# Preparing an LSH-masked attention two head pairs at a time, with one chain of scales and one hash compare for both

## The chip, the cores and the metric

The kernel runs on one core of a Trainium2 chip. That core has a matrix engine (TensorE, PE in the profile; its weight loads are listed apart as PEld), a vector engine (VectorE, DVE), a scalar engine (ScalarE, ACT), a general engine (GpSimd, POOL), and a sync engine (SyncE, SP), from whose queue nearly all transfers are issued, one behind the other. The metric is the time of one execution on the device in microseconds (us); the median of three runs is what counts.

## The reference

Two parts stand one behind the other: attention in which a query sees only the keys of its own hash bucket, and a feed-forward layer on what the attention gives.

```python
q_bits = (np.einsum('bhsd,dk->bhsk', q, proj) > 0)          # B,H,S,D = 4,8,768,64 ; 6 bits
k_bits = (np.einsum('bhsd,dk->bhsk', k, proj) > 0)
mask   = (bucket of q)[:, :, :, None] == (bucket of k)[:, :, None, :]
scores = np.matmul(q, k.transpose(0, 1, 3, 2)) / np.sqrt(64)
scores = np.where(mask, scores, -1000000000.0); scores -= max over keys
attn   = exp(scores) / (sum of exp + 1e-09)
x      = (attn @ v) as [3072, 512]
h      = x @ w_in                                            # 512 -> 2048
g      = np.where(h > 0.0, h, np.exp(np.minimum(h, 0.0)) - 1.0)
out    = g @ w_out                                           # 2048 -> 512
```

q, k, v and proj are float32; w_in and w_out are handed over as 64-bit words, from which the kernel makes float32.

## The kernel before

**Numbers in two halves.** A float32 operand is scaled by a power of two and split into a high and a low float16 part, and a product is made of two or three float16 matmuls. The high part is written by ACT (`scaled`, line 143), the low part by DVE (`rest`, line 152). The power of two comes from the largest squared norm of the tile: ACT makes the squares with their sum (`squares`, line 207), and `powers` turns the maximum over the partitions into an exponent and its reciprocal in four or five DVE operations on one or two columns (lines 186 to 199).

**Pairs, chunks and slots.** The 8 heads of a batch are taken as 4 pairs. A batch has two chunks of 384 queries, so there are 8 chunks of 4 pairs, and a pair of a chunk has 6 score tiles of 128 queries by 768 keys ("slots", 24 to a chunk). A slot is: scores on PE (`s`, line 508; in the start every second one is `so`), their maximum and copy to `pt` on DVE (520), the exponentials of two slots on ACT (536), whose bias `nb` comes from POOL (533), the division and split of the probabilities (`hl`, ACT 143 and DVE 152), a transposing transfer into `PT`. When a pair of a chunk has its six tiles, 36 matmuls `av` (560) multiply with V's halves `vhl`, and ACT and DVE write `x` (569, 570).

**Preparing a pair.** `prep` gives the steps of a group of pairs: load (SP, `kst` and `qst`), squares, scales, split, project. The split writes the halves of K into `natk` and of Q into `nat1q`/`nat2q`, and issues the transposing transfers (K at 328, `O1`/`O2` of Q at 371 and 372). The project step copies K's halves to a second tile (`dup`, line 162), multiplies K or Q with the six hash vectors (`z`, line 286), compares the result with a threshold (`zb`, DVE, line 291), and sends the bits by four or two small transfers beside the transposed halves, where the score matmuls pick them up. K is prepared once per batch, with the batch's first chunk; in the second chunk a group has Q alone. From chunk 1 on a group has two pairs. In batch 0's first chunk, a group is one pair; there the buffers of the pairs are three `Stage`s, the first in buffers of its own, the others in the tail of the large tile `W`, as long as no decoded weight stands there. From then on all pairs share one `natk`, `nat1q` and `nat2q`.

**What sets the order.** The list `due` gives each step a slot at which it is to be written: so many slots ahead of the group's first slot (`PREP`, and `PREP0` in the start), not before the step of the group ahead that frees its buffers. Within a slot, the order in the program is scores, exponentials, due steps, weights, feed-forward. Each engine works its own list in order. The order on PE is as written from slot 30 on; for the others a scheduler places what is ready by its own estimate. `behind_max` ties a small DVE operation behind the last score maximum.

**Feed-forward.** A stream of 16 steps per chunk runs six slots behind the attention: `h` (PE 587), Exp and Relu (ACT 600, 602), their combination (DVE 610), the split of `g` into two halves (`U<-U,sgg`, ACT 143 and DVE 152), the second product `o` (PE 630). When a chunk ends, its three 128x512 results leave PSUM as `W<-o,os` and `W<-o_1556,os` (ACT 143; one by DVE 145) into two output areas, and POOL's queue sends them out. The next chunk's `o` takes the same PSUM banks.

**Weights.** 32 slabs of 128x512 are loaded as 64-bit words, decoded (ACT 143, DVE 468, 469, 479), and their column maximum is gathered on PE (`acc`, line 472). When all 16 of a matrix are there, each slab is split (`W<-W,w0s` and `W<-W,w1s`, ACT 143 and DVE 152). All of it is put between the steps of batch 0, and a decode that would overwrite a spare stage buffer waits until the pair that uses it is through.

## Time and profile before

| | |
|---|---|
| median of 3 runs | 938.73 us (935.84, 938.73, 945.27) |
| span of the profiled execution | 936.1 us; it is the only time that this execution has |
| busy share | PE 87%, DVE 76%, ACT 75%, POOL 10% |
| instructions | 14723 |
| mean granted TensorE clock | 0.933 |
| read from and written to HBM | 35.65 MB and 6.29 MB |

The page of the profile gives busy times, a map of the span in 40 slices, the chain of work that ended last, and the costliest groups of instructions. A group's row has the line, the engine, the operation, what is written from what (partitions x elements and type), the count, the total busy time in us with the mean of one in ns, and the engine's idle time just ahead of it with what ended most of that. A row of a timeline has the start, the duration, the instruction, and in brackets the idle time ahead of it with its releaser. A row of the waits has the engine and its line, the releaser, the total in us, the number of times, the longest. The two batches of numbers at a row's end in the table by stretches are the granted clock, the DMA share and GB/s.

### The profile page before, as it was taken

How to read it: one execution, taken by the hardware profiler on the slowest of the kernel's cores; microseconds unless marked ns; L12 is line 12 of the kernel's file. 1: busy time of each engine (PE TensorE's matmuls, PEld its weight loads, DVE VectorE, ACT ScalarE, POOL GpSimd, SP SyncE). 2: the span in 40 equal slices, each digit the busy share in tenths (PEclk: the TensorE clock that was granted, in tenths of full speed). 3: DMA queues.
4: the chain of work that ended last, by engine and by line, in shares of the span. 5: the costliest groups of instructions: out<-in, count | busy, mean ns of one | idle time of the engine just before them, and what ended most of it. 6: DMA issues, size and time to landing. Idle time of an engine off the chain costs nothing.

```text
span 936.1 us, 14723 instructions
## 1 busy us (share of the span) xinstructions
PE 817.0 (87%) x4975; PEld 419.3 (45%) x4975; DVE 712.8 (76%) x1624; ACT 705.4 (75%) x1277; POOL 97.4 (10%) x145
## 2 busy tenths in 40 slices
PE   2436655899898999999988999999999999999996
PEld 0113222354443555554544554455445555555553
DVE  7899889898975868788975777788888787775332
ACT  5666685898968777878877877789787788775442
POOL 1000000011111110210111010200111102110000
PEclk9956665899998999999999999999999999999998
DMA  9999987669787678798798758697687767665000
GB/s 290 270 220 212 232 223 177 120 131 180 137 144 175 133 119 134 148 158 183 138 194 147 146 99 139 147 174 151 118 182 131 120 119 153 103 108 96 34 1 35
DMA packets 404588, 138.49 MB, mean 148 GB/s; under 512 B 380960, under 2 KB 398880, under 8 KB 404512
## 3 DMA queue, kind: packets, MB, share of 16 engines
q1 hardware_dynamic: 402432, 131.25, 70.8%
q0 software_dynamic: 1920, 6.29, 2.1%
q8 instruction: 39, 0.64, 0.3%
q14 instruction: 37, 0.30, 0.1%
q10 hardware_dynamic: 160, 0.00, 0.0%
HBM read 35.65 MB, written 6.29 MB: 45 GB/s over the span
## 4 chain that ended last, share of the span: by engine, by line
PE 36%; issue 12%; DVE 8%; DMA 6%; ACT 5%; POOL 1%; SPq 1%; POOLq 0%; DVEq 0%; ACTq 0%
PE o L630 12%; PE h L587 11%; PE s L508 6%; PE av L560 5%; DVE pt L520 3%; DMA K<-natk 3%; DVE hl L152 2%; ACT pt L536 1%; POOL nb L533 1%; PE z L286 1%; DMA kst<-in_k_dram 1%; ACT hl L143 1%; DMA PT<-hl 1%; DMA out_dram<-W 1%; ACT U L143 1%
## 5 line engine op out<-in xcount | busy, mean ns | idle before, releaser
L630 PE MATMUL o<-W,U 128*128 128x512 f16 x1152 | 284.4, 384 | 13.3 <-ACT W L143 10.5
L587 PE MATMUL h<-x,W 128*128 128x384 f16 x1536 | 279.9, 326 | 0.0
L536 ACT ACTIVATE pt<-pt,nb,sg 128x768 f32<-128x768 f32 x192 | 195.3, 1020 | 53.4 <-POOL nb L533 52.7
L152 DVE SCALAR_TENSOR_TENSOR hl<-pt,r,hl 128x768 f16<-128x768 f32 x192 | 190.6, 1012 | 15.4 <-ACT hl L143 15.2
L587 PEld LDWEIGHTS <-W 128*128 128x128 f16 x1536 | 147.6, 98 | 111.4 <-issue 10.3
L143 ACT ACTIVATE hl<-pt,r 128x768 f16<-128x768 f32 x192 | 168.3, 925 | 15.5 <-issue 6.7
L520 DVE TENSOR_SCALAR_CACHE_REDUCE pt<-s 128x768 f32<-128x768 f32 x177 | 168.2, 950 | 14.0 <-issue 5.5
L630 PEld LDWEIGHTS <-U 128*128 128x128 f16 x1152 | 111.5, 98 | 137.0 <-issue 21.2
L508 PE MATMUL s<-K,O 128*128 128x384 f16 x708 | 153.6, 340 | 21.7 <-DVE pt L520 14.8
L533 POOL TENSOR_SCALAR nb<-m,sg 128x2 f32<-128x2 f32 x96 | 81.5, 849 | 716.5 <-DVE pt L520 376.9
L152 DVE SCALAR_TENSOR_TENSOR U<-U,sgg 128x384 f16<-128x384 f32 x128 | 78.7, 615 | 70.4 <-ACT U L143 69.7
L508 PEld LDWEIGHTS <-O 76*128 76x128 f16 (+1 forms) x768 | 74.4, 102 | 121.9 <-issue 47.5
L143 ACT ACTIVATE U<-U,sgg 128x384 f16<-128x384 f32 x128 | 77.8, 608 | 59.3 <-DVE U L610 59.3
L560 PE MATMUL av<-PT,vhl 128*64 128x384 f16 x1152 | 111.9, 347 | 11.8 <-DMA PT<-hl 6.4
L560 PEld LDWEIGHTS <-vhl 128*64 128x64 f16 x1152 | 71.2, 116 | 61.2 <-issue 17.5
L610 DVE SCALAR_TENSOR_TENSOR U<-U 128x384 f32<-128x384 f32 x128 | 70.7, 553 | 36.6 <-ACT U L602 36.6
L600 ACT ACTIVATE U<-h,ch 128x384 f32<-128x384 f32 x128 | 72.4, 566 | 32.0 <-PE h L587 31.9
L602 ACT ACTIVATE U<-h,ch 128x384 f32<-128x384 f32 x128 | 72.7, 568 | 0.0
L472 PE MATMUL acc<-W,ones 128*128 128x512 bf16 x32 | 17.6, 557 | 39.2 <-DVE W L469 37.4
L570 DVE SCALAR_TENSOR_TENSOR x<-av,x 128x384 f16<-128x384 f32 x32 | 17.7, 555 | 30.4 <-ACT x L569 30.4
L536 ACT ACTIVATION_READ_ACCUMULATOR pt<-pt,nb,sg 128x1 f32 x192 | 36.4, 190 | 0.0
L291 DVE TENSOR_SCALAR zb<-z,pjt 64x384 f16<-64x384 f32 (+1 forms) x48 | 29.0, 604 | 0.3 <-PE z L286 0.3
(103 smaller groups left out, 521.1 us busy)
## 6 DMA issues: line engine op xcount, KB each, us to landing
U<-in_moe_w_in_dram SPq DMA_DIRECT2D x12, 512.0 KB
vf<-in_v_dram SPq DMA_DIRECT2D x16, 384.0 KB
U<-in_moe_w_out_dram SPq DMA_DIRECT2D x12, 512.0 KB
out_dram<-W POOLq DMA_DIRECT2D x24, 256.0 KB, 3.7
qst<-in_q_dram SPq DMA_DIRECT2D x30, 192.0 KB
kst<-in_k_dram SPq DMA_DIRECT2D x14, 384.0 KB
PT<-hl SPq DMA_TRANSPOSE x192
W<-in_moe_w_in_dram SPq DMA_DIRECT2D x4, 512.0 KB
```

Of the source, the lines that this page charges most:

```text
L143: nc.scalar.activation(o, x, AF.Copy, scale=s)
L152: nc.vector.scalar_tensor_tensor(o, x, s, hi, ALU.mult, ALU.subtract)
L508: nc.tensor.matmul(s_tile[:, n, :HALF], st[o][:rows, at, :], kst[kk][:rows, j * NC + n * HC : j * NC + (n + 1) * HC, :].rearrange("p a b - ...
L520: top = nc.vector.tensor_scalar(pt.rearrange("p (n e) -> p n e", n=2), s_tile[:, :, :HALF], CLAMP, None, ALU.max, ALU.max, accum_out=duo[0 ...
L533: nc.gpsimd.tensor_scalar(nb[:, :w], m[:, :w], st["sg"][:, 1:2], 1.0, ALU.mult, ALU.mult)
L536: nc.scalar.activation(pt, pt, AF.Exp, bias=nb[:, n : n + 1], scale=st["sg"][:, 0:1], accum_out=sm[:, n : n + 1])
L560: nc.tensor.matmul(av[j * D : (j + 1) * D], vt[:, j, c, vx, :], PTs[j][:, :, px, c, :], start=n == 0, stop=n == last,)
L587: nc.tensor.matmul(h, WH[:, g * KT + t, wx, fc * P : (fc + 1) * P], c["xs"][t][:, xx, :], start=n == 0, stop=n == 3 * KT - 1,)
L600: nc.scalar.activation(e, h, AF.Exp, scale=c["ch"])
L602: nc.scalar.activation(hp, h, AF.Relu, scale=c["ch"])
L610: nc.vector.scalar_tensor_tensor(e, e, -1.0, hp, ALU.add, ALU.min)
L630: nc.tensor.matmul(o[t][:, :DO], g16[:, gx, t * P : (t + 1) * P], WH[:, NSI + 1 + f, wx, :], start=f == 0 and i == 0, stop=f == NF - 1 and ...
```

## The change

Four things change in how pairs are prepared.

1. The steps of preparation are regrouped: groups are of two pairs from the start, in batch 0 too, and there are four stages instead of three. Both pairs of a group are split at the same due slot (as far as the ring of three Q buffers lets them), K is still projected pair by pair, Q once for both.
2. K's and Q's scales of a group come from one chain, `qk_scales`: six DVE operations for K and Q of both pairs (five where only Q is prepared), instead of two chains and two products. The factors 2^64 go into the constants; the negative scale is no longer made, POOL multiplies by -1 instead.
3. The hash bits of Q of two pairs are compared in one operation on 128 partitions (before: two on 64). The four small transfers behind it are as before.
4. V's halves are written for two heads in one operation (768 columns, before: two of 384).

```diff
-STAGES = 3
+STAGES = 4
...
-            d = nc.sync.dma_start(o[D : D + 2 * NB, u * w : (u + 1) * w], zb[u * QD : u * QD + 2 * NB])
+            d = nc.sync.dma_start(o[u], zb[u * QD : u * QD + 2 * NB])
...
+        def project():
             w = nc_ * P
+            hi, lo, o = [], [], []
+            for st in sts:
+                o1, o2 = flat(st["O1"]), flat(st["O2"])
+                for u in range(2):
+                    at = slice(u * w, (u + 1) * w)
+                    hi.append(o1[:, at])
+                    lo.append(o2[:D, at])
+                    o.append(o2[D : D + 2 * NB, at])
+            bits(o, ((2, hi), (2, lo), (3, lo)), w, 1)
...
+    def qk_scales(b, ps, mx, kw, ksts, qsts):
+        w = len(ps)
+        n = kw + w
+        mall = small.tile([P, 4], F32, tag="qkm", name="qkm")[:, :n]
+        if kw:
+            t = ps_a.tile([P, 512], F32, tag="av", name="sum")[:, :kw]
+            nc.tensor.matmul(
+                t, ones, mx[:, :kw].bitcast(BF16).rearrange("p (n t) -> p n t", t=2)[:, :, 1], start=True, stop=True
+            )
+            nc.vector.tensor_scalar(mall[:, :kw], t, 4.0, None, ALU.max)
+        nc.vector.tensor_scalar(mall[:, kw:], mx[:, kw:], 4.0, None, ALU.max)
+        ex = small.tile([P, 4], F32, tag="ke" if kw else "qe", name="qke", bufs=4 if kw else 2)[:, :n]
+        nc.vector.tensor_scalar(
+            ex.bitcast(I32), mall.bitcast(I32), 1, 0x7F800000, ALU.logical_shift_right, ALU.bitwise_and
+        )
+        sc = small.tile([P, 4], F32, tag="qks", name="qks")[:, :n]
+        nc.vector.reciprocal(sc, ex)
+        nc.vector.tensor_scalar(sc, sc, 2.0 ** (QK_TOP - 64), None, ALU.mult)
+        sg = small.tile([P, 2], F32, tag="sg", name="sg")
+        c = D**-0.5 * 2.0 ** (128 - 2 * QK_TOP)
+        nc.vector.scalar_tensor_tensor(sg[:, :w], ex[:, kw:], c, kexs[b, ps[0]], ALU.mult, ALU.mult)
...
-            for j in range(2):
-                scaled("v_hi", t[:, j, :, 0, :], f[:, j], st["sc"])
-                rest("v_lo", t[:, j, :, 1, :], f[:, j], st["sc"], t[:, j, :, 0, :])
+            scaled("v_hi", t[:, :, :, 0, :], f, st["sc"])
+            rest("v_lo", t[:, :, :, 1, :], f, st["sc"], t[:, :, :, 0, :])
...
-        nc.gpsimd.tensor_scalar(nb[:, :w], m[:, :w], st["sg"][:, 1:2], 1.0, ALU.mult, ALU.mult)
+        nc.gpsimd.tensor_scalar(nb[:, :w], m[:, :w], st["sg"], -1.0, ALU.mult, ALU.mult)
...
-    groups = [[n] for n in range(NP)] + [[n, n + 1] for n in range(NP, len(pairs), 2)]
+    groups = [[n, n + 1] for n in range(0, len(pairs), 2)]
...
-            at = begin[n] - (PREP0 if early else PREP)[2]
+            at = lead[2]
...
+        a = max(split_at[0], scale_at)
         for i, n in enumerate(ns):
+            a = max(a, split_at[i])
+            due.append((a, n, 2, lambda split=split, i=i: split(i)))
+        z = max(lead[3], a)
+        for i, p in enumerate(projects):
+            due.append((z + i, ns[-1], 3 + i, p))
```

The steps move, and with them what stands between others on each engine. Three places show it; line numbers of the changed kernel are larger by up to 19 in what follows the new function.

The first place is ACT's list at the end of chunk 0 (its feed-forward's last step), from just ahead of the first copy out of PSUM (`W<-o,os`) or a little behind it, to the last (`W<-o_1556` and `W<-o_1494`). `natk,kx<-kst` and `nat1q,qx<-qst` (`qkx` in the changed kernel) are the squares of K and Q of batch 1's first group. Before:

```order
L143 ACTIVATE U<-U,sgg 128x384
L207 ACTIVATE nat1q,qx<-qst 128x384
L600 ACTIVATE U<-h,ch 128x384
L602 ACTIVATE U<-h,ch 128x384
L207 ACTIVATE natk,kx<-kst 128x768
L207 ACTIVATE nat1q,qx<-qst 128x384
L600 ACTIVATE U<-h,ch 128x384
L602 ACTIVATE U<-h,ch 128x384
L143 ACTIVATE hl<-pt,r 128x768 x2
L207 ACTIVATE natk,kx<-kst 128x768
L143 ACTIVATE U<-U,sgg 128x384
L143 ACTIVATE W<-o_1556,os 128x512
```

And of the changed kernel, the same stretch:

```order
L207 ACTIVATE nat1q,qkx<-qst 128x384 x2
L143 ACTIVATE U<-U,sgg 128x384
L143 ACTIVATE hl<-pt,r 128x768 x2
L616 ACTIVATE U<-h,ch 128x384
L618 ACTIVATE U<-h,ch 128x384
L143 ACTIVATE W<-o,os 128x512
L552 ACTIVATE pt,sm<-pt,nb,sg 128x768 x2
L143 ACTIVATE U<-U,sgg 128x384
L616 ACTIVATE U<-h,ch 128x384
L618 ACTIVATE U<-h,ch 128x384
L143 ACTIVATE W<-o_1494,os 128x512
```

K's squares no longer stand between the copies: they come some ten exponentials later, Q's stand ahead of the first copy, and one pair of Exp and Relu and the two `hl` halves have left the stretch.

The second place is SP's queue in the start, from the first pair's transposes to the load of V. `K_209` (`K_204`) and `O_215`, `O_216` (`O_210`, `O_211`) are the first pair's transposed halves, `O_321`, `O_322`, `K_315` (`O_235`, `O_236`, `K_229`) the second pair's, `K_210<-zb` (`K_205`) the first pair's hash bits; `W<-in_moe` and `U<-in_moe` are slabs of weights. Before:

```order
L372 DMA_TRANSPOSE O_216<-nat2q 128x6x128
L371 DMA_TRANSPOSE O_215<-nat1q 128x6x128
L328 DMA_TRANSPOSE K_209<-natk 128x12x128
L456 DMA W<-in_moe_w_in_dram 128x1024
L456 DMA U<-in_moe_w_in_dram 128x1024 x3
L305 DMA kst<-in_k_dram 128x2x384
L372 DMA_TRANSPOSE O_322<-W 128x6x128
L295 DMA K_210<-zb 12x384 x4
L391 DMA vf<-in_v_dram 128x2x384 x4
L456 DMA W<-in_moe_w_in_dram 128x1024
```

And of the changed kernel:

```order
L353 DMA_TRANSPOSE O_211<-nat2q 128x6x128
L320 DMA_TRANSPOSE K_204<-natk 128x12x128
L472 DMA W<-in_moe_w_in_dram 128x1024
L352 DMA_TRANSPOSE O_210<-nat1q 128x6x128
L472 DMA U<-in_moe_w_in_dram 128x1024 x3
L320 DMA_TRANSPOSE K_229<-W 128x12x128
L352 DMA_TRANSPOSE O_235<-W 128x6x128
L353 DMA_TRANSPOSE O_236<-W 128x6x128
L295 DMA K_205<-zb 12x384 x4
L408 DMA vf<-in_v_dram 128x2x384 x4
```

The second pair's three transposes now all stand ahead of the first pair's bits and of V, where one stood before.

The third place is DVE's list in the preparation of a batch with loads from the shared buffers (batch 2's first pair), from K's low half (`natk<-kst`) to the copy of its transposed halves (`K_4220<-K_4219`, then `K_4079<-K_4078`), which can start only when the transposing transfer has landed. Before:

```order
L152 SCALAR_TENSOR_TENSOR natk<-kst,ks,natk 128x12x64
L520 TENSOR_SCALAR pt,m<-s 128x768
L546 TENSOR_SCALAR r<-sm 128x2
L152 SCALAR_TENSOR_TENSOR U<-U,sgg 128x384
L152 SCALAR_TENSOR_TENSOR nat2q<-qst,qs,nat1q 128x6x64
L547 RECIPROCAL r<-r 128x2
L162 COPY nat1q<-nat1q 128x6x64
L520 TENSOR_SCALAR pt,m<-s 128x768
L610 SCALAR_TENSOR_TENSOR U<-U 128x384
L408 TENSOR_REDUCE vx_4260<-vx 128x1
L152 SCALAR_TENSOR_TENSOR hl<-pt,r,hl 128x768 x2
L162 COPY K_4220<-K_4219 64x1536
```

And of the changed kernel:

```order
L152 SCALAR_TENSOR_TENSOR natk<-kst,qks,natk 128x12x64
L536 TENSOR_SCALAR pt,m<-s 128x768
L152 SCALAR_TENSOR_TENSOR nat2q<-qst,qks,nat1q 128x6x64
L162 COPY nat1q<-nat1q 128x6x64
L626 SCALAR_TENSOR_TENSOR U<-U 128x384
L152 SCALAR_TENSOR_TENSOR hl<-pt,r,hl 128x768 x2
L536 TENSOR_SCALAR pt,m<-s 128x768
L162 COPY K_4079<-K_4078 64x1536
```

The split of `g`, the maximum of V and the two small operations on `r` no longer stand between the two.

More of the change, by code (lines that the diff above doesn't have):

```diff
@@ L333, in project @@
             quads = [k1[:, u * HALF : (u + 1) * HALF] for u in range(4)]
-            st["done"] = bits(k2, ((0, quads), (1, quads)), HALF, 0)
-        return load, scale, split, project
+            o = [k2[D : D + 2 * NB, u * HALF : (u + 1) * HALF] for u in range(4)]
+            st["done"] = bits(o, ((0, quads), (1, quads)), HALF, 0)
+        return load, sums, split, project
     def prep_q(b, c0, nc_, ps, ksts, sts, sgs):
@@ L347, in load, with sums @@
                     )
-        def scale():
-            w = len(ps)
-            mx = small.tile([P, 2], F32, tag="qx", name="qx")[:, :w]
+        def sums(mx):
             for n, (st, sg_) in enumerate(zip(sts, sgs)):
                 squares(mx[:, n : n + 1], flat(st["qf"]), sg_.q1[:, : 2 * nc_])
-            yield
-            ex, sc = powers(mx, w, 4.0, QK_TOP, "q", rows=True, squares=True)
-            sg = small.tile([P, 2, 2], F32, tag="sg", name="sg")
-            c = D**-0.5 * 2.0 ** (-2 * QK_TOP)
-            for x in range(2):
-                nc.vector.scalar_tensor_tensor(
-                    sg[:, x, :w], ex, c if x == 0 else -c, kexs[b][:, ps[0] : ps[0] + w], ALU.mult, ALU.mult
-                )
-            for n, st in enumerate(sts):
-                st["qsc"], st["sg"] = sc[:, n : n + 1], sg[:, :, n]
         def split(st, sg_):
@@ L717, in prep @@
         made = []
+        kw = len(ps) if c["c0"] == 0 else 0
         def sums():
-            made.extend(part[1]() for part, _ in parts)
-            for m in made:
-                next(m)
+            mx = small.tile([P, 4], F32, tag="qkx", name="qkx")[:, : kw + len(ps)]
+            made.append(mx)
+            if kw:
+                parts[0][0][1](mx[:, :kw])
+            parts[-1][0][1](mx[:, kw:])
         def scale():
             with behind_max():
-                for m in made:
-                    next(m, None)
+                qk_scales(b, ps, made[0], kw, ksts, [qs[n] for n in ns])
         def split(i):
@@ L731, in split @@
                 part[2](sts[i], sgs[i])
-        def project(x, i):
-            part, sts = parts[x]
-            part[3](sts[i])
-        return load, sums, scale, split, project, len(parts)
+        projects = [lambda st=st: parts[0][0][3](st) for st in ksts] if kw else []
+        projects.append(parts[-1][0][3])
+        return load, sums, scale, split, projects
     due = []
```

45 lines of the change are left out of this document (17 added, 28 removed).

## The prediction

> **What bounds the kernel.** I read the page first, then the table of busy time by stretches, then the waits of PE and DVE, then the timeline where a wait is long. The stretches are the start, and then roughly the feed-forward of each chunk; the columns are busy time (and count) of PE, PEld, DVE, ACT and POOL, then the granted clock, the DMA share and GB/s.
>
> ```profile
> span 936.1 us, 14723 instructions
> ...
> 0.00:165.00 165.00, 84.30 (x374) 34.94 (x375) 145.18 (x370) 108.02 (x192) 9.13 (x39) 0.70 0.93 230
> 165.00:283.00 118.00, 106.62 (x659) 54.15 (x658) 101.03 (x232) 101.68 (x183) 16.62 (x14) 0.96 0.77 145
> 283.00:385.00 102.00, 97.62 (x614) 51.36 (x612) 74.63 (x164) 82.02 (x154) 9.97 (x14) 0.97 0.76 142
> ...
> 690.00:790.00 100.00, 99.81 (x640) 52.78 (x639) 77.70 (x173) 79.31 (x145) 11.57 (x16) 1.00 0.75 139
> 790.00:936.00 146.00, 138.22 (x825) 73.38 (x823) 70.42 (x131) 82.82 (x146) 10.71 (x15) 0.98 0.32 62
> ```
>
> From 283 on PE is busy 96 to 100% of a stretch: PE's work bounds it, and a saving on DVE or ACT moves nothing there unless PE waits for it. In the first 165 us PE is busy for half of the time; DVE is busy 145.18 of 165 and the DMA engines 0.93, so this stretch is bounded by DVE, with the transfers close behind. The stretch from 165 to 283 lies between: PE is without work for 118 - 106.62 = 11.4 us. So a change to the preparation can pay in three places: the start, the first chunk, and single waits of PE later.
>
> ```profile
> PE acc L472 <- DVE W L469: 37.4, 16, 5.8
> ...
> PE o L630 <- ACT W L143: 10.5, 4, 4.6
> ...
> DVE K L162 <- DMA K<-natk: 13.2, 10, 3.5
> ```
>
> The first row is the start (column maxima behind weight decodes). The second is PE waiting for the copy that frees the PSUM bank of `o` when a chunk ends: 10.5 us in four places. The third is DVE standing before the copy of K's transposed halves.
>
> **The change part by part: the ends of chunks 0 and 2 (-11).** The timeline at the end of chunk 0, ACT's and PE's rows:
>
> ```profile
> 283.88 0.67 ACT L143 ACTIVATE W<-o,os 128x512 f32<-128x512 f32 x1
> ...
> 288.63 0.84 ACT L207 ACTIVATE natk<-kst 128x768 bf16<-128x768 f32 x1
> 288.84 1.46 PE L630 MATMUL o<-W,U 128*128 128x512 f16 x6
> ...
> 290.90 1.75 ACT L143 ACTIVATE hl<-pt,r 128x768 f16<-128x768 f32 x2
> 292.55 0.83 ACT L207 ACTIVATE natk<-kst 128x768 bf16<-128x768 f32 x1
> 293.88 0.67 ACT L143 ACTIVATE W<-o,os 128x512 f32<-128x512 f32 x1
> 294.61 2.72 PE L630 MATMUL o<-W,U 128*128 128x512 f16 x6 [4.30 <-ACT W L143]
> 297.25 4.16 PE L560 MATMUL av<-PT,vhl 128*64 128x384 f16 x36
> ```
>
> ACT makes four squares, four Exp and Relu and two `hl` halves between its two copies, so the second comes 10 us behind the first, and PE stands for 4.30 us. The six matmuls behind it take 2.72 us where six take 1.46 otherwise, and the 36 `av` 4.16 where a chain row has 3.05:
>
> ```profile
> 292.00:294.00 2.00, 0.00 (x0) 0.00 (x0) 1.81 (x2) 2.00 (x5) 0.00 (x0) 0.65 1.13 243
> 294.00:296.00 2.00, 1.39 (x4) 0.55 (x4) 0.73 (x2) 2.00 (x4) 0.59 (x1) 0.50 0.48 109
> 296.00:298.00 2.00, 2.00 (x10) 0.61 (x9) 0.00 (x0) 1.97 (x5) 0.00 (x0) 0.50 0.42 145
> ...
> 345.81 3.05 PE av L560 x36
> ```
>
> The granted clock falls to 0.50 behind the wait: 1.26 us lost on `o` and 1.11 on `av`. At the end of chunk 2 the same stands, here because the square waits for its load:
>
> ```profile
> 492.64 0.84 ACT L207 ACTIVATE natk<-kst 128x768 bf16<-128x768 f32 x1 [1.84 <-DMA kst<-in_k_dram]
> ...
> 498.11 2.72 PE L630 MATMUL o<-W,U 128*128 128x512 f16 x6 [4.61 <-ACT W L143]
> ```
>
> Together 4.30 + 1.26 + 1.11 + 4.61 + 1.26 = 12.5 us. In the changed order K's squares come behind the last copy, and what is left between the copies is one pair of exponentials, one of Exp and Relu, one split. That is what the kernel before has at the end of chunk 1:
>
> ```profile
> 385.16 0.68 ACT L143 ACTIVATE W<-o,os 128x512 f32<-128x512 f32 x1
> ...
> 391.33 0.69 ACT L143 ACTIVATE W<-o,os 128x512 f32<-128x512 f32 x1 [0.85 <-DMA out_dram<-W]
> ...
> 392.07 1.45 PE L630 MATMUL o<-W,U 128*128 128x512 f16 x6 [0.26 <-ACT W L143]
> ```
>
> There the copies are 6.2 us apart, PE waits 0.26 us, and `o` runs at full speed. The fourth of the waits, at the end of chunk 3, is 10.5 - 4.30 - 4.61 - 0.26 = 1.33. I put these two, 1.6 us together, in the place of the two that go: -11. Its bounds are -12.5 and 0 (if something else takes the gap).
>
> The clock is where a page can be weighed. The Trainium skill ("TensorE: Matmul & The Clock Gate", "Part 1: The HAM clock gate") says that TensorE drops to half rate when it was idle over a window of about 3.4 us, and needs about as long of work to come back; the fall from 1.00 through 0.65 to 0.50 behind a 4.30 us wait agrees. By that rule a new wait of 2 us would cost its 2 us only, one of 4 us would cost 2.4 more, as in the rows.
>
> **The start (+3).** Two pairs are loaded, scaled and split before the first is projected. In SP's queue one transpose of K and one of Q are put ahead of V's loads and of the first pair's bits:
>
> ```profile
> 30.24 2.98 SPq L328 DMA_TRANSPOSE K<-W  x1
> ...
> 32.77 0.16 DVE L408 TENSOR_REDUCE vx<-vx 128x1 f32<-128x4 f32 x1 [2.92 <-ACT W L207]
> ...
> 35.27 1.24 SPq L371 DMA_TRANSPOSE O<-W  x1
> ...
> 35.42 0.13 PEld L508 LDWEIGHTS <-O 76*128 76x128 f16 x2 [6.77 <-DMA O<-zb]
> ...
> L610 DVE SCALAR_TENSOR_TENSOR U<-U x128: 527/553/559, 173.6 to 923.6; 128x384 f32<-128x384 f32 x128
> ```
>
> That is 2.98 + 1.24, some 4 us, on a chain that already keeps DVE idle for 2.92 at V's maximum and PE for 6.77 at the first scores. Against this stands that the work is not more: summing the durations of DVE's list in the two orders up to the first combination of Exp and Relu (L610, at 173.6 before) gives 181.2 us before and 181.3 after (durations by kind; rows overlap a little, so that the sum is more than the time). 26 weight splits stand ahead of it instead of 16, and far fewer small operations. If the later idle time absorbs the 4 us, the start costs nothing, and DVE's 19.8 us of idle time in the first stretch leave room for a gain; if V and the first scores push each other, it is twice that. I take +3 in a range of -3 to +8.
>
> **The first chunk (-5).** The ten splits that are now done earlier are off the first chunk:
>
> ```profile
> L152 DVE SCALAR_TENSOR_TENSOR W<-W,w1s 128x512 f16<-128x512 f32 x16 | 11.9, 744 | 2.3 <-ACT W L143 2.3
> L143 ACT ACTIVATE W<-W,w1s 128x512 f16<-128x512 f32 x16 | 11.4, 713 | 1.3 <-DVE W L152 1.2
> ```
>
> 10 x 0.744 = 7.4 us of DVE and 7.1 of ACT, and summing the lists up to the 16th combination gives 9.8 us less on DVE (279.4 to 269.6) with the small operations. ACT is busy 101.68 and DVE 101.03 of 118 us, so some 6/7 of these would be seen if they alone set the pace; PE's 106.62 us of work allow at most 11.4. I take -5, half of the saving, with 0 and -9 as ends.
>
> **Small operations, compares and V beside PE (0).**
>
> ```profile
> L198 DVE RECIPROCAL qs<-qe 128x2 f32<-128x2 f32 (+1 forms) x18 | 2.9, 159 | 0.0
> L291 DVE TENSOR_SCALAR zb<-z,pjt 64x384 f16<-64x384 f32 (+1 forms) x48 | 29.0, 604 | 0.3 <-PE z L286 0.3
> L152 DVE SCALAR_TENSOR_TENSOR vhl<-vf,vs,vhl 128x384 f16<-128x384 f32 x32 | 18.7, 609 | 0.0
> L152 DVE SCALAR_TENSOR_TENSOR natk<-kst,ks,natk 128x768 f16<-128x768 f32 x14 | 14.1, 1009 | 0.7 <-ACT natk L143 0.7
> ```
>
> 88 of 176 scale operations go, at 0.07 us (the spacing in which they start) to 0.16 us: 6 to 14 us. 16 of 48 compares go: 9.7 us. V's 32 low halves become 16 of the width of `natk`'s, 18.7 - 16 x 1.009 = 2.6 us. That is about 20 us of DVE, but all except the start's share lies beside a PE that is 96 to 100% busy: nothing, unless the cover is gone, and then at most some 15. The merged V operation holds DVE for 1.009 us at once instead of 0.609. On the Trainium skill's page "Perfetto Trace Analysis" ("Optimizing Scalar/DVE Operations") the grouping of operations pays when the engine is saturated, and where it is not but causes gaps elsewhere, smaller pieces are said to let work end sooner; by that, the 12 merged operations of the later batches could cost 12 x 0.4 = 4.8 us, and I take 0, since no row of PE's waits names V's halves.
>
> **The copies of K (-1).** Before the copy, DVE waits for the transposed halves:
>
> ```profile
> 412.17 1.00 DVE L152 SCALAR_TENSOR_TENSOR natk<-kst,ks,natk 128x768 f16<-128x768 f32 x1
> ...
> 417.12 1.46 SPq L328 DMA_TRANSPOSE K<-natk  x1
> ...
> 422.17 0.55 DVE L162 COPY K<-K 64x1536 f16<-64x1536 f16 x1 [3.49 <-DMA K<-natk]
> ```
>
> Here the low half was done at 412.17 + 1.00 = 413.17, but SP issued the transpose 3.9 us later, behind other items, and it landed 5 us after. In the changed lists the transpose of K stands first behind the split, which takes up to 3.9 us off; but the work that DVE does in between falls from 6.2 to 7.2 us to 5.0 to 5.9, so that a wait of the same length shows 1.2 us more. Bounds: -5 (half of the 13.2 gone and passed on to PE) and +20 (below); -1 is near nothing.
>
> **The sum**: +3 - 5 - 11 - 1 + 0 = -14 on the span of 936.1, so 922.1. The median of the runs shown is 2.6 above that span (938.73), and put to the median it is 924.7, **925 us**, 1.5% faster.
>
> **The rivals.**
> - *The start eats its gain.* Loads, transposes and V of two pairs come at once on DMA engines that are 0.93 busy, the first combination is 10 us later and the first chunk gives nothing back: 936.1 + 10 - 11 = 935, or 937 to 938 on the median. For it: the 6.77 us wait for the bits, which now stand behind two transposes more. Against: DVE has no more work up to there. Chance 0.18.
> - *The wait at the chunk's end is replaced.* The last copy waits for its output area or ACT for POOL's `nb`, and PE again stands for 3 to 4 us with a cold clock behind it; the boundaries give 3 instead of 11: 930.1, on the median 933. For it: 0.85 us of the 391.33 copy was a wait for the output area. Chance 0.14.
> - *Slower: the copies of K pass their waits to PE.* Three batches with shared buffers have 12 copies. DVE does its list in order, and behind each copy stand a maximum of a score tile and the compare; if each waits 1.2 to 2.2 us more than before and PE's score bank is not free meanwhile, that is 14 to 26, say 20 us: 936.1 + 20 - 11 = 945.1, 948 on the median, and 959 where the boundaries stay as well. It decides from about 1.5 us per copy. Against: the transpose comes earlier by up to 3.9 us. Chance 0.09.
> - *All of it pays.* DVE bounds the start outright, so that the 36 small operations fewer, the compares and V there (some 7.6 us by the same sum) come off, the first chunk runs without gaps (-9), the boundaries give 12.5: 907, 910 on the median. Chance 0.09.
>
> **How the numbers follow.** The forecast has the remaining 0.50, with its own range of 916 to 934 (its start from -3 to +8, its chunk from 0 to -9, not all at once). The range of 8 in 10 reaches from 911, half of the last rival, to 940, beyond the first two: 911 to 940. About 1% is what a measurement of this kernel can tell from no change, that is 929.3 and 948.1. Faster by more: 0.44 of the forecast's 0.50, the last rival's 0.09, and 0.07 of the first two: 0.60. Slower by more: half of the third rival and a start that is worse than its range: 0.08. Within 1%: 0.32.
>
> **What the profile after would show.** PE's row of waits for `W` L143 falls from 10.5 to 2 or 3 us in total, without a granted clock of 0.50 after the first chunk. The first scores with both halves stand at some 39 to 42 us instead of 35.4, the first combination 0 to 8 us later than 173.6, the stretch of the first chunk is shorter by 5. DVE's busy time falls by about 20 us, PE's wait in the steady stretches does not. DVE's waits for K's transpose stay within 8 to 18 us in total. What would make the prediction wrong: a new row of PE's waits above 10 us in the steady chunks (K's copies, POOL's `nb`, `PT`), or a first combination behind 184 us.

## The result, and the profile after

Over 17 runs the changed kernel takes 946.6 us (941.97 to 950.42), the kernel before 940.83 (935.84 to 945.27): the ratio is 1.005, 95% interval 1.0035 to 1.0066. The change made the kernel half a per cent slower, where 925 us and faster was forecast; the time lies outside the range of 911 to 940. The profiled execution's span is 945.3 us, 9.2 above the span before, while the medians are 5.8 apart: the execution of the kernel before that was profiled is some 3 us below that kernel's median. Single executions of one kernel differ by up to 8 or 9 us, so that a difference of 1 to 3 us in one chunk, from one trace each, is a reading and no more.

The table by stretches of the changed kernel, with the same edges and columns as before, then the row of the first combination of Exp and Relu, and last the fourth stretch of the kernel before:

```profile
0.00:165.00 165.00, 68.89 (x316) 25.47 (x317) 135.07 (x309) 100.14 (x175) 7.69 (x38) 0.76 0.86 215
165.00:283.00 118.00, 99.89 (x624) 53.38 (x625) 97.33 (x203) 99.57 (x174) 14.09 (x15) 0.91 0.81 151
283.00:385.00 102.00, 99.66 (x661) 54.32 (x657) 77.19 (x167) 82.83 (x156) 12.69 (x15) 1.00 0.76 147
385.00:487.00 102.00, 94.22 (x605) 50.93 (x604) 81.80 (x174) 83.88 (x151) 15.91 (x15) 0.98 0.83 163
...
L626 DVE SCALAR_TENSOR_TENSOR U<-U x128: 535/552/559, 192.5 to 932.8; 128x384 f32<-128x384 f32 x128
...
385.00:487.00 102.00, 96.95 (x631) 51.30 (x628) 84.60 (x199) 85.31 (x155) 15.90 (x16) 1.00 0.82 157
```

In the first 165 us DVE is busy for 135.07 instead of 145.18, and the DMA share is 0.86 instead of 0.93: the stretch that DVE bounded now has 10 us more in which DVE waits. The third row is what was hoped for: PE is busy 99.66 of 102 where it was 97.62. The fourth went the other way, 94.22 against 96.95. The edges are the same, but the changed kernel is up to 19 us behind in its work, so that a stretch doesn't hold quite the same steps.

The feed-forward makes the place of each gain and loss easy to read. DVE's combination (L610 before, L626 after) runs 16 times per chunk; the table has the start of the first one, and the time from one chunk's first combination to the next's (the last chunk's to its own last):

| | first | chunk 0 | 1 | 2 | 3 | 4 | 5 | 6 | 7 |
|---|---|---|---|---|---|---|---|---|---|
| before | 173.6 | 105.9 | 101.5 | 102.5 | 101.6 | 100.2 | 94.1 | 85.8 | 58.4 |
| after | 192.5 | 100.2 | 96.1 | 104.6 | 95.1 | 103.4 | 96.6 | 85.8 | 58.4 |
| difference | +18.9 | -5.7 | -5.4 | +2.1 | -6.5 | +3.2 | +2.5 | 0 | 0 |

The differences add up to 9.1 of the 9.2 us. Three of the forecast's terms can be read off: chunk 0 gave 5.7 (forecast: 5), chunks 1 and 3, which begin with the ends of chunks 0 and 2, gave 11.9 together (forecast: 11). The start lost 18.9 (forecast: 3), and chunks 2, 4 and 5 lost 7.8 (forecast: 1 gained).

PE's waits in the changed kernel, and two rows of the kernel before:

```profile
PE av L576 <- DMA PT<-hl: 28.2, 12, 5.6
PE so L524 <- DVE pt L536: 10.6, 8, 2.9
PE sum L184 <- DVE vx L425: 9.9, 1, 9.9
PE z L286 <- DMA O<-W: 9.4, 2, 9.0
PE z L286 <- DMA K<-W: 8.5, 2, 8.2
PE av L576 <- DVE zb L291: 7.1, 4, 2.1
...
PE o L646 <- ACT W L143: 1.9, 3, 0.7
...
PE av L560 <- DMA PT<-hl: 6.4, 6, 1.7
...
PE av L560 <- DVE zb L291: 0.5, 1, 0.5
```

The row of `o` is the chunk ends: 1.9 us where 10.5 stood. The first and the sixth are much larger than before (6.4 and 0.5); the third, fourth and fifth are the start. Most of the first lies in the start and chunk 0 as well: 19.8 of its 28.2 us lie ahead of 283 us, and 8.4 us in four places, two in chunk 2 and two in chunk 4.

**The start.** The timeline from the first pair's hash bits to the first score maximum, SP's queue, DVE and PE, and below it three rows of the kernel before:

```profile
20.15 5.20 SPq L320 DMA_TRANSPOSE K<-W  x1
...
25.40 2.77 SPq L352 DMA_TRANSPOSE O<-W  x1
...
28.27 1.23 SPq L353 DMA_TRANSPOSE O<-W  x1
...
29.60 3.22 SPq L295 DMA_DIRECT2D K<-zb  x4
...
32.87 2.05 SPq L408 DMA_DIRECT2D vf<-in_v_dram  x4
...
34.09 0.62 DVE L291 TENSOR_SCALAR zb<-z,pjt 128x384 f16<-128x384 f32 x1 [1.51 <-DMA K<-zb]
...
36.58 4.80 SPq L295 DMA_DIRECT2D K<-zb  x4
...
42.75 0.16 DVE L425 TENSOR_REDUCE vx<-vx 128x1 f32<-128x4 f32 x1 [8.04 <-ACT W L207]
...
43.10 3.90 SPq L295 DMA_DIRECT2D O<-zb  x4
...
47.18 0.82 PE L524 MATMUL s<-K,O 76*128 76x384 f16 x2 [1.36 <-DMA O<-zb]
...
52.63 0.95 DVE L536 TENSOR_SCALAR_CACHE_REDUCE pt<-s 128x768 f32<-128x768 f32 x1
```

```profile
20.64 3.22 SPq L295 DMA_DIRECT2D K<-zb  x4
...
23.91 2.71 SPq L391 DMA_DIRECT2D vf<-in_v_dram  x4
...
36.51 0.95 DVE L520 TENSOR_SCALAR_CACHE_REDUCE pt<-s 128x768 f32<-128x768 f32 x1
```

The second pair's three transposes hold SP's queue from 20.15 to 29.50. Behind them the first pair's bits of K, ready since 20.7, go out at 29.60 (20.64 before), V's loads at 32.87 (23.91 before). V's maximum comes 10 us later, and DVE, which works its list in order, stands 8.04 us in front of it. The bits of Q are compared by 34.71, but go out only at 43.10: in SP's queue stand loads of weights and the second pair's bits of K (36.58 to 41.38) ahead of them, and some of these sends wait until a load of V or of weights has landed. The scores have Q's bits at 47.18 (35.42 before), and then DVE's list still has V's halves and the next group's splits ahead of the first maximum, at 52.63 instead of 36.51.

### The profile page after: what moved, and what is told of

It is laid out like the page before. It is cut to its first block, busy times and chain, and to the rows that moved or that the text cites. A ratio compares the mean times of both kernels' runs of the same rounds, so it can differ in the third digit from the quotient of the medians.

```text
span 945.3 us, 14573 instructions
## 1 busy us (share of the span) xinstructions
PE 800.1 (85%) x4973; PEld 419.8 (44%) x4973; DVE 705.0 (75%) x1504; ACT 702.9 (74%) x1261; POOL 109.2 (12%) x146
## 5 line engine op out<-in xcount | busy, mean ns | idle before, releaser
L646 PE MATMUL o<-W,U 128*128 128x512 f16 x1152 | 278.8, 379 | 2.6 <-ACT W L143 1.9
L549 POOL TENSOR_SCALAR nb<-m,sg 128x2 f32<-128x2 f32 x96 | 93.2, 971 | 723.2 <-DVE pt L536 452.7
L524 PE MATMUL s<-K,O 128*128 128x384 f16 x708 | 150.8, 336 | 8.6 <-DVE pt L536 4.4
L576 PE MATMUL av<-PT,vhl 128*64 128x384 f16 x1152 | 113.3, 347 | 41.1 <-DMA PT<-hl 28.2
L524 PEld LDWEIGHTS <-O 128*128 128x128 f16 (+1 forms) x768 | 74.7, 102 | 99.6 <-issue 39.3
L576 PEld LDWEIGHTS <-vhl 128*64 128x64 f16 x1152 | 74.6, 116 | 85.2 <-issue 39.7
L626 DVE SCALAR_TENSOR_TENSOR U<-U 128x384 f32<-128x384 f32 x128 | 70.6, 551 | 36.2 <-ACT U L618 36.2
L488 PE MATMUL acc<-W,ones 128*128 128x512 bf16 x32 | 16.8, 554 | 33.0 <-DVE W L485 32.2
L143 ACT ACTIVATE W<-U 128x512 f32<-128x512 f32 x24 | 15.8, 663 | 22.8 <-DMA U<-in_moe_w_out_dram 12.6
```

The costliest lines, as they stand in the source:

```text
L143: nc.scalar.activation(o, x, AF.Copy, scale=s)
L524: nc.tensor.matmul(s_tile[:, n, :HALF], st[o][:rows, at, :], kst[kk][:rows, j * NC + n * HC : j * NC + (n + 1) * HC, :].rearrange("p a b - ...
L549: nc.gpsimd.tensor_scalar(nb[:, :w], m[:, :w], st["sg"], -1.0, ALU.mult, ALU.mult)
L576: nc.tensor.matmul(av[j * D : (j + 1) * D], vt[:, j, c, vx, :], PTs[j][:, :, px, c, :], start=n == 0, stop=n == last,)
L626: nc.vector.scalar_tensor_tensor(e, e, -1.0, hp, ALU.add, ALU.min)
L646: nc.tensor.matmul(o[t][:, :DO], g16[:, gx, t * P : (t + 1) * P], WH[:, NSI + 1 + f, wx, :], start=f == 0 and i == 0, stop=f == NF - 1 and ...
```

## The experiments

All were run beside the kernel before; ratios are to it. The kernel before had medians from 940.65 to 945.57 us in these sets of runs, so that a small difference between two experiments is better read from their ratios. "End of chunk 0" is the first combination of chunk 1: 279.5 us before, 292.7 after, so 13.2 us are lost up to there.

**1. Batch 0 pair by pair.**

```diff
-STAGES = 4
+STAGES = 3
-    groups = [[n, n + 1] for n in range(0, len(pairs), 2)]
+    groups = [[n] for n in range(NP)] + [[n, n + 1] for n in range(NP, len(pairs), 2)]
```

(For a group of two that follows groups of one, the product of the scales is made per pair, and the ring of the exponents has six buffers instead of four.)

> The changed kernel with one edit undone: batch 0's first chunk is prepared pair by pair again, with three stages; one chain of scales, the joint compare of Q from chunk 1 on and V's joint parts stay. Theory A (the 18.9 us that the start lost come from the second pair's three transposes, which stand in SP's queue ahead of V's loads and of the first pair's hash bits): V's maximum is back near 33 us (42.75 in the changed kernel, 32.77 before), the first combination of Exp and Relu near 174 to 178 us (192.54, 173.62), and the time 14 to 18 us below the changed kernel's 946.6, about 930, which is also below the kernel before. Rival B (the longer operations of V, or the scales in one chain, keep DVE in the start): the first combination stays at 185 us or later and the time at 942 to 948.

934.4 us, ratio 0.9918 (0.9892 to 0.9944): 12 us below the changed kernel, and faster than the kernel before. V's maximum is at 33.70, the first score maximum at 42.69; the first combination is at 184.8, where Rival B had it rather than Theory A, but the end of chunk 0 is at 285.5, 7.2 earlier than in the changed kernel, and the time is below all that Rival B allowed. So grouping by two in the start is the larger part of what is lost up to the end of chunk 0, but 6 us against the kernel before are left there.

**2. V's loads ahead of the second pair's transposes.**

```diff
-                with tc.issue_after(ks[b, V_AFTER]["done"].ins) if b == 0 else nullcontext():
+                with tc.issue_after(ks[b, V_AFTER]["first"].ins) if b == 0 else nullcontext():
```

> The changed kernel, with V's loads of batch 0 put into SP's queue behind the first pair's transposes and ahead of the second pair's, nothing else. Theory A1 (V's late loads are what the start lost, since DVE stands before V's maximum with its list in order): V's maximum comes 8 to 10 us earlier than 42.75, the first combination 8 to 12 us earlier than 192.54, the time 935 to 939. Rival A2 (the hash bits behind the transposes are what is late; V's loads only add to the queue ahead of them): V's maximum is early, but the first score maximum stays at 50 to 56 us and the time within 3 us of 946.6.

946.7 us, ratio 1.004 (1.0021 to 1.0059).

```profile
28.62 0.16 DVE L425 TENSOR_REDUCE vx<-vx 128x1 f32<-128x4 f32 x1 [4.04 <-ACT W L207]
...
46.51 0.82 PE L524 MATMUL s<-K,O 76*128 76x384 f16 x2 [7.44 <-DMA O<-zb]
...
49.01 0.95 DVE L536 TENSOR_SCALAR_CACHE_REDUCE pt<-s 128x768 f32<-128x768 f32 x1
```

V's maximum comes 14 us earlier, and yet the first scores wait for the bits of Q until 46.51. The time is Rival A2's: the late V alone is not what the start lost. In this trace the first combination is 7.4 us earlier (185.2) and the end of chunk 0 5.2 us (287.6), but the profiled execution is the shortest of ten, and the median shows nothing of it; whether the late V has a part in the loss stays open.

**3. Q compared pair by pair in batch 0.** The edit lets Q's project step take one pair, and puts the steps of the start in the order K, Q, K, Q.

> The changed kernel, with Q projected and compared pair by pair in batch 0's first chunk (K, Q, K, Q instead of K, K, Q for both); groups of two pairs, the joint scales, splits and loads stay. Theory I (the first pair's Q bits, which the first scores need, are late because the joint compare has to wait for the second pair's Q; issued at 43.10 in the changed kernel): the bits go out before 40 us, the first score maximum comes at 42 to 47 us instead of 52.63, the first combination 5 to 10 us earlier than 192.54, the time 937 to 942. Rival J (they wait in SP's queue behind the second pair's transposes and V's loads anyway, and DVE stands before V's maximum): the first score maximum stays above 49 us, the time within 3 us of 946.6.

946.3 us, ratio 1.0039 (1.0016 to 1.0062).

```profile
36.52 1.85 SPq L295 DMA_DIRECT2D O<-zb  x2
...
45.78 0.82 PE L524 MATMUL s<-K,O 76*128 76x384 f16 x2 [0.27 <-DMA O<-zb]
```

The first pair's bits of Q go out 6.6 us earlier than 43.10, but the scores have them at 45.78 instead of 47.18: they land 9 us after they were sent, behind V's loads and three loads of weights that went out just ahead, from 32.96 to 36.47. The first score maximum comes at 47.61, between what Theory I and Rival J had, the end of chunk 0 2.7 us earlier; the time is Rival J's. The bits come late, compared jointly or not, and here it is not only SP's queue that holds them, but what is still on its way when they are sent.

**4. The second pair split behind the first pair's projects**, with joint loads, squares, scales and V as in the changed kernel. Core of the edit, for batch 0 alone (steps split, K, Q, split, K, Q in the place of split, split, K, K, Q):

```diff
+            for i in range(len(ns)):
+                projects.append((2.5 + i, lambda i=i: split(i)))
+                projects.append((3, lambda i=i: parts[0][0][3](ksts[i])))
+                projects.append((4, lambda i=i: parts[-1][0][3]([qs[ns[i]]])))
...
+                due.append((z + (0, 1, 1, 2, 3)[i], ns[0], 3 + i, p))
```

> The changed kernel, where in batch 0's first chunk the second pair of a group is split only behind the first pair's K and Q projects, and Q is projected pair by pair; loads, squares and scales of both pairs stay joint, V's parts too. The second pair's three transposes then stand behind V's loads and the first pair's bits in SP's queue, as with pairs prepared alone. Theory Q (the place of these transposes is what the start lost; the joint loads and scales cost nothing): V's maximum near 33, the first score maximum at 42 to 44, the end of chunk 0 at 285 to 287 as with pairs prepared alone, the time 933 to 937. Rival R (the joint loads, squares and scales of two pairs cost the start as well): the end of chunk 0 stays at 289 or later, the time at 940 or above.

935.1 us, ratio 0.9916 (0.9887 to 0.9944). SP's queue, PE and DVE in its start:

```profile
21.58 3.48 SPq L295 DMA_DIRECT2D K<-zb  x4
25.10 4.22 SPq L408 DMA_DIRECT2D vf<-in_v_dram  x4
...
29.88 0.76 SPq L295 DMA_DIRECT2D O<-zb  x1
...
31.24 0.76 SPq L295 DMA_DIRECT2D O<-zb  x1
32.04 2.25 SPq L320 DMA_TRANSPOSE K<-W  x1
...
35.09 0.16 DVE L425 TENSOR_REDUCE vx<-vx 128x1 f32<-128x4 f32 x1 [2.68 <-ACT W L207]
...
36.43 0.96 DVE L536 TENSOR_SCALAR_CACHE_REDUCE pt<-s 128x768 f32<-128x768 f32 x1
```

The first pair's bits of K and Q and V's loads are all out before the second pair's transposes, and the first score maximum is where it was before the change (36.51). The end of chunk 0 is at 282.9, 9.8 us earlier than in the changed kernel, and it stays to the end (10.6 us in the spans, 11.5 in the medians). Theory Q holds; Q's compare apart is part of the edit, and left the time as it was by itself (experiment 3). The first combination, at 181.9, is still 8.3 us later than before the change, and at the end of chunk 0 3.5 us are left; which of the joint loads, scales and V's parts these belong to isn't shown.

**5. Project steps one slot earlier from chunk 1 on.**

```diff
-PREP = (18, 14, 10, 5)
+PREP = (18, 14, 10, 6)
```

On the changed kernel:

> The changed kernel, with the project steps from chunk 1 on due one slot earlier (PREP's last number 6 instead of 5), so that Q's joint compare no longer falls into the slot in which the probabilities are multiplied with V. Theory C (the waits of PE before av for zb, 7.1 us in four places, come from Q's project being the third step in a row, since both take the same PSUM bank): this row falls to 1 us or less, and the time by 4 to 7 us to 940 to 943. Rival D (av then waits for something else that is as late, such as PT, or the project waits for its transposes on PE): the row falls, another of PE's rows rises by as much, and the time stays within 2 us of 946.6.

942.6 us, ratio 0.9998 (0.9974 to 1.0022). The row falls from 7.1 to 3.1 us, that for `PT` rises from 28.2 to 33.7, nearly all of it ahead of chunk 1 (the four waits in chunks 2 and 4 are 8.6 us, 8.4 without the edit). Chunks 2, 4 and 5 are 2.6, 0.8 and 3.3 us shorter, chunk 3 is 3.3 longer. The time is Theory C's. The same number in the kernel of experiment 1:

> The kernel with batch 0 prepared pair by pair (934.4 us), with the project steps from chunk 1 on due one slot earlier. In the changed kernel the same edit took PE's wait before av for zb from 7.1 to 3.1 us and the time to 942.6. Theory C (that wait is Q's joint compare in the slot of av): the row falls from 8.0 to 3 us or less, the time to 929 to 932. Rival K (what it gained there lay in the start by chance of the order): the time stays at 933 to 937.

927.1 us, ratio 0.9857 (0.9828 to 0.9887), 0.6% below experiment 1's. The row of experiment 1, and of this kernel:

```profile
PE av L582 <- DVE zb L291: 8.0, 6, 1.9
...
PE av L582 <- DVE zb L291: 3.4, 3, 1.6
```

Chunks 2 and 4 take 98.4 and 98.5 us (101.5 and 101.2 in experiment 1). Here Theory C holds for the wait: the matmuls `z` in front of the compare and `av` take the same single PSUM buffer, and Q's joint compare, third step in a row, fell into the slot of `av`. The row explains 4.6 us of the gain; where the rest comes from isn't shown. And the edits of this experiment and the fourth together on the changed kernel:

> Two edits together on the changed kernel: in batch 0 the second pair is split behind the first pair's projects (alone: 946.6 to 935.1), and the project steps from chunk 1 on are due one slot earlier (alone: 946.6 to 942.6). Theory S (the first is the start, the second PE's waits before av for zb in chunks 1 to 5; two places, so they add): 929 to 932, with chunks 2 and 4 at 102 or less (104.6 and 103.4 in the changed kernel). Rival T (what the second edit gave alone was the start's order): 934 to 937.

935.4 us, ratio 0.9899 (0.9868 to 0.993), not clearly less than experiment 4 alone (0.9916). Against experiment 4, chunks 2 and 4 gain 1.9 and 1.6 us, chunks 1 and 3 lose 2.8 and 1.8. The two edits don't add.

**6. Splits from chunk 1 on, earlier and later.** The second pair at its own slot again, on the changed kernel:

```diff
-            at = lead[2]
+            at = lead[2] if early else begin[n] - PREP[2]
```

> The changed kernel, with the second pair of a group from chunk 1 on split at its own slot again (ten slots ahead of its own first slot, as before the change). Theory E (the waits of PE before av for PT, 28.2 us against 6.4 before, come from the transposes of the second pair's K and of the first pair, which stand together in SP's queue just ahead of the last PT of a pair): this row falls to about 12 us or less, and the time by 6 to 10 us to 936 to 941. Rival F (they come from the first pair's transposes alone, which stay, or from batch 0): the row stays above 20 us and the time within 3 us of 946.6.

957.8 us, ratio 1.0168 (1.014 to 1.0197): the wrong way. The row for `PT` stays at 26.7 us, but most of it lies ahead of chunk 1. Of the four waits in chunks 2 and 4 (8.4 us), the second of each chunk goes or shrinks (2.24 to none, 2.39 to 0.61), while the first stays (2.01 and 1.86). So Theory E names the cause of half of them, but its time falls: chunk 1 grows by 3.9 us, chunks 3 and 5 by 1.5 and 1.8. In this kernel, that both pairs are split together from chunk 1 on is a gain. All splits one slot earlier (11 for 10), in the kernel of experiment 1 with earlier projects:

> Batch 0 prepared pair by pair and project steps one slot earlier (alone together: 927.1), and in addition the splits of a group from chunk 1 on due one slot earlier (11 instead of 10), so that the first pair's transposes are further ahead of the last PT before av in SP's queue. Theory U (PE's waits before av for PT, 1.2 to 1.6 us in four places at the start of chunks 2 to 5, come from the first pair's transposes just ahead in SP's queue): those four waits fall below 0.6 us and the time by 4 to 6 us to 921 to 924. Rival V (the transposes then push another PT or the hash bits): the four waits fall, others come up, the time stays at 925 to 930.

928.7 us, ratio 0.9832 (0.9805 to 0.9858), the same as without it within the intervals (0.9857). Of the four waits for `PT` at `av`, 1.0 to 1.4 us each are left, where 1.2 to 1.6 stood. The time is Rival V's: one slot earlier for all splits doesn't take these waits away.

**7. V's parts per head again.**

```diff
-            scaled("v_hi", t[:, :, :, 0, :], f, st["sc"])
-            rest("v_lo", t[:, :, :, 1, :], f, st["sc"], t[:, :, :, 0, :])
+            for j in range(2):
+                scaled("v_hi", t[:, j, :, 0, :], f[:, j], st["sc"])
+                rest("v_lo", t[:, j, :, 1, :], f[:, j], st["sc"], t[:, j, :, 0, :])
```

In the kernel of experiment 1:

> The kernel with batch 0 prepared pair by pair (934.4 us, first combination at 184.8, end of chunk 0's feed-forward at 285.6), with V's halves written per head again. Theory G (V's joint operations hold DVE and ACT in the start, where every us of DVE counts, 1.0 us at a time): chunk 0's end comes 3 to 6 us earlier, the time 929 to 932. Rival H (V's joint parts save a little there, since DVE is full and 16 x 0.609 x 2 is more than 16 x 1.009; the rest of the start's loss is the order of the small chain): chunk 0's end within 2 us, the time 933 to 938.

926.7 us, ratio 0.9853 (0.9831 to 0.9876), 7.7 us less than experiment 1 (6.1 by the ratios); the first combination at 173.2, the end of chunk 0 at 280.1, where of the 6 us that were left in experiment 1 0.6 remain. In the changed kernel:

> The changed kernel, with V's halves written per head again, nothing else. With batch 0 prepared pair by pair the same edit gave 7.7 us (934.4 to 926.7). Theory N (V's joint operations cost 6 to 8 us wherever they stand, since they hold a DVE and an ACT that others wait for): the end of chunk 0 comes 4 to 6 us earlier than 292.7, the time 938 to 941. Rival O (that gain belonged to the order with pair by pair; here the second pair's transposes set the start): the end of chunk 0 within 2 us, the time 944 to 948.

944.2 us, ratio 1.0013 (0.999 to 1.0037), 2.4 us less (3.5 by the ratios). The end of chunk 0 comes 4.4 us earlier, as Theory N had it, while the time is Rival O's. The joint parts put into the kernel before:

> The kernel before, with V's halves written for both heads in one operation, nothing else. Theory N (the joint operations cost 6 to 8 us wherever they stand): the time 5 to 9 us above the kernel before, ratio 1.005 to 1.010, lost in the start and chunk 0 above all. Rival P (they only cost beside the one chain of scales, or what V apart gained was another order of small things): within 3 us of the kernel before.

941.7 us, ratio 0.9989 (0.9969 to 1.0009), no difference. And with experiment 1 and earlier projects:

> Three edits together: batch 0 prepared pair by pair, V's halves per head, project steps from chunk 1 on one slot earlier. Alone beside the first, the second gave 7.7 us and the third 7.3 us. If they add, the time is 918 to 921; if the second is an accident of the order in the start, it is 924 to 930.

932.6 us, ratio 0.9884 (0.9841 to 0.9926), 5.5 us more than with V joint in the medians, 2.5 by the ratios, whose intervals overlap. So V's parts per head gain 6 to 8 us in one surrounding, 2 to 4 in another, and nothing that can be told in two: there is no single price of the joint operation to be had from it. What sets the difference, the order that the scheduler makes around it or something else, isn't settled.

**8. The ends of chunks 0 and 2 by themselves**, in the kernel before:

```diff
-PREP = (18, 14, 10, 5)
+PREP = (18, 12, 10, 5)
```

> The kernel before, with one number changed: the squares of a group from chunk 1 on are due two slots later (PREP's second number 12 instead of 14), so that one square of K is left between the copies at the end of chunk 0 and none at the end of chunk 2, where two of K and two of Q stood. Theory L (the two ends cost the kernel before about 12 us, by ACT's squares between its copies): PE's waits for W from ACT's line 143 fall from 10.5 to 4 us or less, chunks 1 and 3 of the feed-forward are each 4 to 6 us shorter than 101.5 and 101.6, the time falls by 8 to 12 us to 929 to 934. Rival M (the waits move to what then comes later, such as the scales and the split of K): chunks 1 and 3 shorten, chunks 2 and 4 lengthen by as much, the time within 3 us of the kernel before.

948.3 us, ratio 1.0073 (1.0047 to 1.0099).

```profile
PE sum L184 <- DVE zb L291: 13.7, 6, 2.9
...
PE o L630 <- ACT W L143: 4.7, 3, 2.6
```

The wait at the ends falls from 10.5 to 4.7 us, and chunks 1 and 3 shorten by 3.6 and 2.8, but chunks 2 and 4 grow by 6.5 and 8.8. PE waits 13.7 us in six places for a compare ahead of the matmul over the partitions that the scales need, which now comes later. Rival M holds for this way of moving the squares, at a higher price than it had (7.7 us above the kernel before). The change moved them without that.

## Why the prediction was wrong

**The step that failed is the start (+3 in a range of -3 to +8; it was +18.9).** Of the 23 us between the forecast for the span (-14) and what it did (+9.2), 16 are the start, and 9 are chunks 2, 4 and 5, which the sum had at -1 together. The prediction's own sign of being wrong, a first combination behind 184 us, came (192.5). Two things in the start's working were wrong.

First, the size of the hold in SP's queue. The prediction counted one transpose of K and one of Q, 2.98 + 1.24, from rows of the kernel before. The two that are new ahead of the bits (K at 20.15, O at 25.40; the third has its like there before the change too) take 5.20 and 2.77 us, 8.0 instead of 4.2. SP's queue has no gap of a microsecond between its items from 16 to 42 us, and the bits of K and V's loads go out 9.0 us later. Why this transpose of K takes 5.20 us isn't shown: the share of the DMA engines is 1.01 in its stretch, and 1.08 in that of the 2.98. What came behind was not counted at all: Q's bits, ready at 34.71, stand in the queue until 43.10.

Second, "the work up to there is not more" was taken as an argument that the idle time would be absorbed. DVE is busy 152.2 us up to the first combination before, and 157.4 after: 5 us more, with 26 instead of 16 weight splits done by then, and 35.1 instead of 21.5 us idle. The sum of durations is nearly the same (180.1 and 181.3 us), as the prediction had it; it counts overlapping rows twice. And the idle time was not absorbed: DVE works its list in order, and what stood behind V's maximum was all late. Experiment 4 shows that the place of the second pair's split is the larger part of the cause: it takes back 9.8 of the 13.2 us at the end of chunk 0, with loads, squares, scales and V's parts joint. The cause of the other 3.5 is open. The first rival ("the start eats its gain") named the mechanism, the bits behind two transposes more, and priced the start at +10 with no gain in chunk 0, near the 13.2 us that the two cost together, and 937 to 938 in all.

**The first chunk (-5)** was right in its size (-5.7), but it is no gain apart from the start: the splits that are off chunk 0 were done ahead of it. In the first kernel of experiment 7, with 16 splits ahead of the first combination and that at 173.2 again, chunk 0 takes 106.8 us, as much as before. That the size came out is in part luck.

**The ends of chunks 0 and 2 (-11)** were right, -11.9, with PE's wait for the copies at 1.9 us. (That wait fell by 8.6 us, and the prediction's rows had 3.6 us more for the slow matmuls behind it.) The copies at the end of chunk 0 are 5.9 us apart:

```profile
297.98 0.68 ACT L143 ACTIVATE W<-o,os 128x512 f32<-128x512 f32 x1
...
303.85 0.69 ACT L143 ACTIVATE W<-o,os 128x512 f32<-128x512 f32 x1 [0.93 <-DMA out_dram<-W]
...
304.85 1.47 PE L646 MATMUL o<-W,U 128*128 128x512 f16 x6
```

No square is between them, the second waits for its output area as at the end of chunk 1 before, and `o` runs at full speed behind it. That the length of chunks 1 and 3 is due to this alone is read from the traces; experiment 8, meant to show it, moved other things too.

**The small operations, compares and V beside PE (0)** is the second term that failed: chunks 2, 4 and 5 lost 7.8 us. DVE's busy time fell by 7.9 us (712.8 to 705.0), not by 20. By their own rows the parts fell as worked out: the compares by 9.5 (29.0 to 19.5), V by 2.5 and the scales' small operations by 8.6 (21.7 to 13.1). But rows on DVE overlap: their sum fell by 24.6 us, their overlap by 16.8. The joint compare had a price that was not looked for, a place in PE's order: K is projected twice and Q behind it, in three due slots, one after the other, and the third step met `av` in the one PSUM buffer that they share.

```profile
426.97 3.09 PE L576 MATMUL av<-PT,vhl 128*64 128x384 f16 x35 [1.95 <-DMA PT<-hl]
...
455.01 3.19 PE L576 MATMUL av<-PT,vhl 128*64 128x384 f16 x36 [1.63 <-DVE zb L291]
...
480.39 4.79 PE L576 MATMUL av<-PT,vhl 128*64 128x384 f16 x35 [2.24 <-DMA PT<-hl]
```

These are chunk 2's; chunk 4 has the same three, chunks 1 and 5 one wait for `zb` each. Experiment 5 takes the waits for `zb` in chunks 2 and 4 away and gains 6 to 7 us in the kernel of experiment 1. On the changed kernel 4 us go, of which the chunks show only a part. The waits for `PT` are explained in part: the second of a chunk goes or shrinks when the second pair is split at its own slot (experiment 6). What sets the first, and why all four are 1.2 to 1.4 us in experiment 1 and 1.8 to 2.4 here, is open.

**The copies of K (-1)** held: DVE's wait for the transposed halves went from 13.2 to 8.4 us, so the slower rival (20 us by the copies) didn't come, and the slower outcome came by the start instead.

On the clock, the third of the `av` rows above shows more than the prediction allowed. `av` takes 4.79 instead of 3.09 us behind a wait of 2.24 us, and the granted clock there falls:

```profile
478.00:480.00 2.00, 0.15 (x1) 0.00 (x0) 2.00 (x6) 2.00 (x4) 1.73 (x1) 1.00 1.13 212
480.00:482.00 2.00, 1.61 (x16) 1.04 (x18) 1.18 (x3) 0.79 (x2) 1.26 (x1) 0.79 1.07 223
482.00:484.00 2.00, 2.00 (x16) 1.16 (x14) 0.59 (x2) 1.93 (x5) 0.00 (x0) 0.50 0.96 284
```

The length of the wait alone doesn't decide it. A wait of 2.39 us at 680.64 in the same kernel cost nothing, and in the first kernel of experiment 5 one of 1.88 us was followed by 0.50 as well:

```profile
680.64 3.08 PE L576 MATMUL av<-PT,vhl 128*64 128x384 f16 x35 [2.39 <-DMA PT<-hl]
...
628.44 4.79 PE L576 MATMUL av<-PT,vhl 128*64 128x384 f16 x35 [1.88 <-DMA PT<-hl]
...
630.00:632.00 2.00, 2.00 (x16) 1.12 (x14) 0.88 (x2) 1.86 (x6) 0.00 (x0) 0.50 0.97 356
```

In a trace's records the granted clock changes only at the edges of equal steps of 3.41 us (here it is 0.50 from 481.18 to 484.59). PE's idle time can be counted in each step that began at full clock, behind 283 us, in all 16 traces. In 23 steps it was 1.97 us or more, and the clock fell at the end of every one; in 66 it was 1.2 to 1.96 us, and the clock fell behind two of them (1.71 and 1.88). The wait of 2.24 us lies within one step; that of 2.39 is cut by an edge at 679.15 into 0.90 and 1.49. By the reading of the Trainium skill ("TensorE: Matmul & The Clock Gate", "Part 1: The HAM clock gate") in the prediction, a wait of 2 us costs its 2 us only; here the measurement decides otherwise, one such wait cost 2.24 + 1.7 us.

## What to carry to other kernels

Joining two preparations into one saved operations here, but it also put the second one's transfers ahead of what the first one's consumer waits for. In a queue that works in order, count everything that moves ahead, leave room in its price (a transpose of K held SP's queue for 2.25 to 5.20 us at different moments of the start), and let the second half go behind the first one's last send: here that was worth 11 us, and it made a version that is 0.8% faster than the kernel before out of one that is 0.5% slower. The best versions measured, 926.7 to 928.7 us (ratios 0.983 to 0.986), keep the joint scales and, from chunk 1 on, the joint compares, and prepare the first chunk of batch 0 pair by pair.

## What the runs showed that was not expected

Edits of a few instructions moved this kernel by up to 8 us, and by amounts that depend on what else was changed: V's parts per head gave 6 to 8 us in one kernel, 2 to 4 in another and nothing clear in two, and one slot for the projects 4 to 5 us in one, 6 to 7 in another and nothing clear in a third. Two edits that gain 7.7 and 7.3 us beside a third gain 1.8 together (934.4 to 932.6; by the ratios 0.65% and 0.61%, and 0.34% together). Traces whose chunk 0 ends 3 to 5 us earlier (experiments 2 and 3, and 7 on the changed kernel) showed 0 to 2.4 us in the medians. And half of the clock was lost behind waits of PE of 1.88 and 2.24 us, while one of 2.39 us cost nothing.
